# Strided attention products and softmax normalisations of chunks 2 to 4 on VectorE instead of GpSimd

## The chip, the cores and the metric

One core of a Trainium2 chip runs the kernel. The metric is the device time of one execution in microseconds (us). The engines are named as in the profile: PE is TensorE's matmul, PEld its weight load, DVE is VectorE, ACT is ScalarE, POOL is GpSimd, SP is SyncE, which here only issues DMAs.

## The reference

Three layers follow one another, all in 32-bit floats.

```python
# q, k, v: (4 batches, 8 heads, 576 positions, 64)
scores = scale * q @ k^T
mask_local   = (rel >= 0) & (rel < 32)                      # heads 0 to 3
mask_strided = (rel >= 0) & (pos_k % 32 == pos_q % 32)      # heads 4 to 7
attn = softmax(where(mask, scores, -1e9));  x = attn @ v    # x: (2304, 512)
g = x @ w_gate
x = (silu(g) * (x @ w_val)) @ w_out                         # 512 -> 1536 -> 512
h = max(x @ w1, x @ w2, x @ w3)                             # 512 -> 768
out = h @ w_out2                                            # 768 -> 512
```

A position of a strided head sees the positions of its own residue modulo 32 alone, at most 18 of them. With the 32 residues and the 4 heads laid over the 128 partitions, row i of a batch (i from 0 to 17) needs i+1 dot products of length 64 on each partition and then a weighted sum of i+1 vectors of length 64.

## The kernel before

**Chunks and slots.** The 2304 tokens are 72 rows of 32 positions. They are cut into five chunks of 15, 15, 14, 14 and 14 rows (480 or 448 tokens), called chunks 0 to 4. The gated layer runs chunk after chunk, and in each over twelve blocks f of 128 hidden columns. One (chunk, f) pair is a slot, written (c, f) here, 48 in all. A slot does a gate product (12 matmuls into the PSUM tile `ps_g`), a value product (12 into `ps_v`) and, one slot late, the output product of the slot before (into `ps_y`). Operands are split into a high and a low part (`hi`, `lo`; `xh`, `xl`; `hh`, `hl`), and a product is three matmuls.

**What a slot asks of the other engines.** ACT takes the tanh of `ps_g` (L524). DVE makes `ht` from it (L525) and multiplies it with `ps_v` (L532). ACT copies out the high part `hh` (L135), POOL subtracts for the low part `hl` (L138). `ps_g` and `ps_v` share two PSUM buffers (`gv`), so that the gate product of the next slot can start only when L525 of this slot has read `ps_g`, and the next value product only when L532 has read `ps_v`.

**The attention of the next chunk runs beside it.** `attention_steps(c)` gives lists of steps, and the main loop places list i of chunk c in slot 12(c-1)+i-3 (chunk 1: in slot i). There are two kinds of work:

- Blocks (class `Block`): local heads, and the first rows of the strided heads of batches 0 and 1, on PE, with a softmax (`softmax`): score, running minimum on DVE (L311), exponential on ACT (L315), sum and reciprocal on DVE (L318, L319), and the normalisation by `norm_eng` (L320). Then PE transposes the normalised tile (L325) and multiplies it with v (L339). Chunks 2 to 4 have four blocks each.
- Units (class `Unit`): the strided rows that are not on PE, in groups of up to six rows. For each row, `qk` multiplies k with the row's q (L416, into the tile `pr`), and DVE sums over the 64 columns (L419, into `stsc`). After the softmax of the unit, `pv` multiplies v with the weights (L438, into `pr`), and DVE sums (L441, into `sto`). `pr` has two buffers, `stsc` one. Chunk 1 has 2 such rows, chunks 2, 3 and 4 have 14 each, 42 together. A row of index i is a product over 64(i+1) columns, 64 to 1152.

`eng` names the engine of L416, L438 and of `norm_eng` at L320. It is DVE for chunk 1 and POOL for chunks 2 to 4.

**Other work in the same stretch.** In chunk 0 the weights of the gated layer are read as 64-bit words and converted to 32-bit floats (`convert`: L158, L159 on ACT, L160 on POOL, L161 on POOL or DVE, L162 and L163 on DVE) and split (L138). In slots of chunks 1 to 4 the weights of the last layers are converted and combined in the same way (`pair_steps`: L195 to L198, L207), paced by the list `PACE`. After slot (4, 9) the last two layers begin; the changed code has no part in them.

**Order.** The instructions of an engine stand in one queue and run in that order. A framework sorts them when the program is made, by program order and by when it expects each to be ready; the waits on semaphores then hold them to the data. Nothing in the diff names an order.

Of the kernel before, what the change touches and what calls it, by code (L numbers as in the profile page):

```python
# [59 lines left out]
def tile_attention_swiglu_maxout(  # L60
# [18 lines left out]
    nc = tc.nc  # L79
# [269 lines left out]
    def local_block(g, early=False):  # L349


        def dst(src):
            for c, i0, i1, o in pieces(LR * g[0], LR * (g[-1] + 1)):
                t, w = slice(i0 * STRIDE, i1 * STRIDE), slice(o * STRIDE, (o + i1 - i0) * STRIDE)
                xh, xl = x_tile(c)
                yield xh[:, 0:2, t], xl[:, 0:2, t], src[:, :, w]

        src = (earq if early else locq, lock, locv)
        return Block(src, (g[0] if early else g[0] - EARLY, g[0]), KB, [mask[0 if n % (NI // LR) == 0 else 1] for n in g], dst, early)

    def strided_block(srcs, b, g, early=False):

        _, rows, nr = ON_PE[b]

        def dst(src):
            for u, n in enumerate(g):
                r0 = min(n * nr, STRIDE - nr)
                su = src[:, :, u * QB:u * QB + nr * rows].rearrange("p a (r i) -> p a r i", i=rows)
                for c, i0, i1, o in pieces(b * NI, b * NI + rows):
                    def part(t):  # L370
                        t = t[:, 2:4, :width(c)].rearrange("p a (i r) -> p a r i", r=STRIDE)
                        return t[:, :, r0:r0 + nr, i0:i1]

                    xh, xl = x_tile(c)
                    yield part(xh), part(xl), su[:, :, :, o:o + i1 - i0]

        return Block(srcs, (g[0], g[0]), rows * nr, [smask[b]] * len(g), dst, early)

    def pairs(ns):
        ns = list(ns)  # L380
        return [ns[i:i + 2] for i in range(0, len(ns), 2)]
# [80 lines left out]
    def attention_steps(c):  # L462

        steps = [[] for _ in range(15)]
        a, b = ROWS[c], ROWS[c + 1]
        eng = nc.vector if c == 1 else nc.gpsimd
        blocks = [local_block(g) for g in pairs(g for g in range(-(-a // LR), -(-b // LR)) if g >= EARLY)]
        if a <= NI < b and len(ON_PE) > 1:
            blocks += [strided_block((st1q, st1k, st1v), 1, g) for g in pairs(range(-(-STRIDE // ON_PE[1][2])))]
        at = [0, 0, 4, 4, 8] if len(blocks) < 6 else [0, 0, 2, 2, 4, 4, 6, 6, 8]  # L470
        for n, blk in enumerate(blocks):
            s0 = at[n]
            steps[max(0, s0 - 2)].append(blk.load)
            steps[s0].append(lambda blk=blk: (blk.scores(), blk.softmax(eng)))
            steps[s0 + 1].append(lambda blk=blk: blk.transpose(nc.scalar))
            steps[s0 + 2].append(blk.pv)
        units = []
        on_pe = {n: rows for n, rows, _ in ON_PE}
        i = a
        while i < b:  # L480
            if i % NI < on_pe.get(i // NI, 0):
                i += 1
                continue
            n = min(6 - i % NI % 6, b - i)
            units.append(Unit(i // NI, i % NI, n))
            i += n
        s0 = 0
        for u in units:
            steps[s0].append(u.load)
            steps[s0].append(u.begin)  # L490
            for r in range(u.n):
                steps[s0 + (2 * r // u.n)].append(lambda u=u, r=r: u.qk(r, eng))
            steps[s0 + 2].append(u.softmax)
            for r in range(u.n):
                steps[s0 + 2 + (2 * r // u.n)].append(lambda u=u, r=r: u.pv(r, eng))
            for r in range(0, u.n, 3):
                steps[s0 + 5 + r // 3].append(lambda u=u, r=r: u.out(r))
            s0 += 4
        return steps
# [254 lines left out]
    if True:  # L754
# [26 lines left out]
        for c in range(1, NC):  # L781
            for i, st in enumerate(attention_steps(c)):
                fill.setdefault(i if c == 1 else (c - 1) * NF + i - 3, []).extend(st)
# [183 lines left out]
```

## Time and profile before

| | |
|---|---|
| median of 3 runs | 852.52 us (851.6 to 852.91) |
| the profiled execution | 851.26 us, of which 849.5 us are the span from its first to its last instruction |
| mean granted clock of TensorE | 0.992 |
| busy share of the span | PE 95%, PEld 83%, DVE 63%, ACT 39%, POOL 46% |
| chunk 0's slots | about 40 to 162 us |
| chunks 1, 2, 3 | begin at about 162, 278 and 374 us |
| chunk 4, then the last layers | begin at about 474 and 565 us |

A busy share is a mean over stages that differ. PE's busy time includes the latency of pipelined matmuls, so that a stretch in which PE stands at 100% can still hold short stalls. The profile tells for each instruction how long its engine sat idle before it, and which engine's instruction ended that idle time.

### The profile page before, as it was taken

What the parts mean: (1) busy time and instruction counts of PE and PEld (TensorE: products, weight loads), DVE (VectorE), ACT (ScalarE), POOL (GpSimd) and SP (SyncE); (2) the same over time, 40 slices, a digit from 0 to 9 for tenths busy, and PEclk for the clock granted to TensorE, in tenths of its full rate; (3) what the DMA queues carried; (4) which work ended last, traced back from release to release, by engine and by line L of the source; (5) the groups of instructions that cost most, each with busy time, mean ns of one, the idle gap of its engine ahead of it and who ended that gap; (6) DMA issues with size and microseconds to landing.
All of it is one profiled execution on the core that took longest, in us unless ns stands there. A gap on an engine that the chain in (4) does not pass through costs nothing.

```text
span 849.5 us, 12626 instructions
## 1 busy us (share of the span) xinstructions
PE 805.3 (95%) x4392; PEld 708.8 (83%) x4392; DVE 538.2 (63%) x1072; ACT 331.4 (39%) x811; POOL 387.7 (46%) x343
## 2 busy tenths in 40 slices
PE   4799899879999999999997999989999999999997
PEld 3677667658888989989896999889999899989986
DVE  3989999977675878847999553633645244524340
ACT  4867476343433443434232242422244123512220
POOL 0355455786666768755987343520313021302110
PEclk9899999989999999999999999999999999999999
DMA  8679778976865889858586996597766375644502
GB/s 234 216 223 378 235 250 292 399 243 220 285 207 164 276 311 305 286 187 287 175 261 226 316 328 213 178 351 320 247 239 219 132 277 225 219 189 148 212 0 75
DMA packets 73915, 202.72 MB, mean 239 GB/s; under 512 B 8716, under 2 KB 38472, under 8 KB 70268
## 3 DMA queue, kind: packets, MB, share of 16 engines
q1 hardware_dynamic: 73852, 201.92, 69.9%
q8 instruction: 35, 0.57, 0.3%
q14 instruction: 28, 0.23, 0.1%
HBM read 160.21 MB, written 41.68 MB: 238 GB/s over the span
## 4 chain that ended last, share of the span: by engine, by line
PE 68%; DVE 13%; DMA 6%; ACT 4%; POOL 4%; issue 4%; SPq 1%; DVEq 0%; ACTq 0%; POOLq 0%
PE ps_a L613 13%; PE ps_z L686 8%; PE ps_c L613 7%; PE ps_g L504 4%; PE ps_g L505 4%; PE ps_y L506 4%; PE ps_g L506 4%; PE ps_y L505 4%; PE ps_y L504 4%; PE ps_v L505 4%; PE ps_v L506 4%; PE ps_v L504 4%; PE ps_b L613 3%; POOL pr L416 2%; DVE w L162 2%
## 5 line engine op out<-in xcount | busy, mean ns | idle before, releaser
L138 POOL TENSOR_TENSOR hl<-t,hh 128x384 fp32r<-128x384 f32 x36 | 37.5, 1045 | 207.7 <-ACT hh L135 161.0
L504 PE MATMUL ps_g<-xh,wh_g 128*128 128x448 f32 (+1 forms) x240 | 94.2, 392 | 7.2 <-DVE ht L525 6.8
L138 POOL TENSOR_TENSOR hl<-ht,hh 128x448 fp32r<-128x448 f32 (+1 forms) x48 | 60.7, 1265 | 82.2 <-ACT hh L135 70.5
L613 PE MATMUL ps_a<-yhT,wr 128*128 128x384 f32 x324 | 94.4, 338 | 0.6 <-ACT s L627 0.6
L504 PE MATMUL ps_v<-xh,w_v 128*128 128x448 f32 (+1 forms) x240 | 89.7, 374 | 1.6 <-DVE stat L311 1.4
L505 PE MATMUL ps_g<-xl,wh_g 128*128 128x448 f32 (+1 forms) x240 | 89.6, 373 | 1.7 <-DVE xl L347 1.7
L506 PE MATMUL ps_g<-xh,wl_g 128*128 128x448 f32 (+1 forms) x240 | 89.9, 375 | 1.1 <-DVE wl_g L138 1.1
L506 PE MATMUL ps_v<-xh,w_v 128*128 128x448 f32 (+1 forms) x240 | 90.2, 376 | 0.0
L505 PE MATMUL ps_v<-xl,w_v 128*128 128x448 f32 (+1 forms) x240 | 89.1, 371 | 0.0
L160 POOL TENSOR_SCALAR raw<-raw 128x512 f32<-128x512 f32 x60 | 53.5, 893 | 61.6 <-ACT w L158 49.7
L627 ACT ACTIVATE s<-ps_a 128x384 f32<-128x384 f32 x81 | 39.3, 490 | 99.0 <-PE ps_a L613 96.1
L438 POOL TENSOR_TENSOR pr<-stv,stsc 128x832 f32<-128x832 f32 (+17 forms) x42 | 67.4, 1624 | 21.4 <-DVE sto L441 9.9
L416 POOL TENSOR_TENSOR pr<-stk,stq 128x832 f32<-128x832 f32 (+17 forms) x42 | 70.6, 1699 | 12.7 <-DVE sto L441 7.1
L506 PE MATMUL ps_y<-hh,w_o 128*128 128x448 f32 (+1 forms) x192 | 71.2, 371 | 0.0
L505 PE MATMUL ps_y<-hl,w_o 128*128 128x448 f32 (+1 forms) x192 | 71.0, 370 | 0.0
L504 PE MATMUL ps_y<-hh,w_o 128*128 128x448 f32 (+1 forms) x192 | 68.0, 373 | 0.0
L686 PE MATMUL ps_z<-wo2t,hh 128*128 128x512 f32 x216 | 64.8, 392 | 0.9 <-ACT osb L695 0.7
L135 ACT ACTIVATE hh<-ht 128x448 fp32r<-128x448 f32 (+1 forms) x48 | 28.0, 584 | 94.6 <-DVE ht L532 89.0
L524 ACT ACTIVATE ht<-ps_g 128x448 f32<-128x448 f32 (+1 forms) x60 | 33.1, 551 | 74.0 <-PE ps_g L506 70.2
L613 PEld LDWEIGHTS ps_a<-yhT,wr 128*128 128x128 f32 x324 | 59.7, 188 | 1.6 <-ACT s L627 1.0
L525 DVE SCALAR_TENSOR_TENSOR ht<-ht,ps_g 128x448 f32<-128x448 f32 (+1 forms) x60 | 37.6, 626 | 34.1 <-ACT ht L524 34.1
L504 PEld LDWEIGHTS ps_g<-xh,wh_g 128*128 128x128 f32 x240 | 45.3, 189 | 16.1 <-DVE ht L525 9.6
(133 smaller groups left out, 1956.5 us busy)
## 6 DMA issues: line engine op xcount, KB each, us to landing
wr<-wsdr SPq DMA_DIRECT2D x27, 1792.0 KB, 7.4
raw<-in_w_dram SPq DMA_DIRECT2D x60, 512.0 KB, 5.4
w_v<-wvdr SPq DMA_DIRECT2D x48, 512.0 KB, 4.4
w_o<-wodr SPq DMA_DIRECT2D x48, 512.0 KB, 4.7
wsdr<-whi SPq DMA_DIRECT2D x27, 256.0 KB, 3.9
wvdr<-w_v SPq DMA_DIRECT2D x12, 512.0 KB, 5.0
wodr<-w_o SPq DMA_DIRECT2D x12, 512.0 KB, 6.3
wsdr<-w SPq DMA_DIRECT2D x18, 256.0 KB, 4.1
```

The lines of the kernel that those rows point to most:

```text
L138: return a.ins, lo_eng.tensor_tensor(lo, src, f32(hi), ALU.subtract).ins
L160: nc.gpsimd.tensor_scalar(f32(hi), f32(hi), -0.0, 1.0, ALU.mult, ALU.mult)
L416: eng.tensor_tensor(pv, self.k[:, 0:i + 1, :], self.q[:, r:r + 1, :].to_broadcast([128, i + 1, D]), ALU.mult)
L438: eng.tensor_tensor(pv, self.v[:, :, 0:i + 1], self.sc[:, r:r + 1, 0:i + 1].to_broadcast([128, D, i + 1]), ALU.mult)
L504: nc.tensor.matmul(ps, wh, xh, start=first, stop=False)
L505: nc.tensor.matmul(ps, wh, xl, start=False, stop=False)
L506: nc.tensor.matmul(ps, wl, xh, start=False, stop=last)
L524: nc.scalar.activation(t, ps[:, :n], AF.Tanh, scale=0.5)
L525: nc.vector.scalar_tensor_tensor(t, t, 1.0, ps[:, :n], ALU.add, ALU.mult)
L613: nc.tensor.matmul(ps, wts[:, c, a, ks], y[k][b], start=first and k == q == 0, stop=k == 1 and q == 2, skip_group_check=True,)
L627: nc.scalar.activation(s, self.a, AF.Copy)
L686: nc.tensor.matmul(z[j], a[:, ts], w[:, f, b], start=f == q == 0, stop=f == NF2 - 1 and q == 2)
```

## The change

`eng` is DVE for every chunk. The products L416 and L438 of the 42 strided rows of chunks 2 to 4, 84 instructions, and the normalisations L320 of their twelve blocks go from POOL's queue to DVE's. Data, tiles and the number of instructions stay the same.

```diff
     def attention_steps(c):
 
         steps = [[] for _ in range(15)]
         a, b = ROWS[c], ROWS[c + 1]
-        eng = nc.vector if c == 1 else nc.gpsimd
+        eng = nc.vector
```

The steps that use it:

```python
steps[s0].append(lambda blk=blk: (blk.scores(), blk.softmax(eng)))
...
steps[s0 + (2 * r // u.n)].append(lambda u=u, r=r: u.qk(r, eng))
steps[s0 + 2].append(u.softmax)
...
steps[s0 + 2 + (2 * r // u.n)].append(lambda u=u, r=r: u.pv(r, eng))
```

## Rows read from the trace of the kernel before

**Rows 1.** The page's head: the span; busy us, share and instructions by engine.

```profile
span 849.5 us, 12626 instructions
PE 805.3 (95%) x4392; PEld 708.8 (83%) x4392; DVE 538.2 (63%) x1072; ACT 331.4 (39%) x811; POOL 387.7 (46%) x343
```

**Rows 2.** Stretches A, M, B: length, busy us (instructions): PE, PEld, DVE, ACT, POOL; clock; DMA.

```profile
151.10:199.60 48.50, 41.39 (x210) 31.50 (x209) 42.47 (x81) 16.95 (x51) 39.95 (x28) 0.93 0.85 302
199.60:407.20 207.60, 207.60 (x1154) 184.95 (x1153) 147.07 (x324) 81.02 (x212) 139.33 (x123) 1.00 0.77 251
407.20:474.40 67.20, 61.91 (x309) 54.90 (x308) 58.33 (x70) 19.23 (x42) 52.94 (x35) 1.00 0.72 238
```

**Rows 3.** What PE waited for, whole span: us in total, times, longest.

```profile
PE ps_g L504 <- DVE ht L525: 6.8, 9, 1.7
```

**Rows 4.** Timeline in slot (1, 7): start, us, engine, line; idle before, its releaser.

```profile
237.34 0.57 ACT L524 ACTIVATE ht<-ps_g 128x480 f32<-128x480 f32 x1 [2.76 <-PE ps_g L506]
237.95 0.65 DVE L525 SCALAR_TENSOR_TENSOR ht<-ht,ps_g 128x480 f32<-128x480 f32 x1 [1.27 <-ACT ht L524]
...
242.53 0.38 PE L504 MATMUL ps_g<-xh,wh_g 128*128 128x480 f32 x1
```

**Rows 5.** Timeline in slot (3, 8).

```profile
441.04 0.55 ACT L524 ACTIVATE ht<-ps_g 128x448 f32<-128x448 f32 x1 [0.59 <-PE ps_g L506]
...
441.86 4.65 POOL L438 TENSOR_TENSOR pr<-stv,stsc 128x832 f32<-128x832 f32 x2 [0.60 <-DVE stsc L431]
...
442.46 2.19 DVE L163 CUSTOM_DVE_ANT_0 w<-w,q 128x1024 uint16<-128x1024 uint16 x1
...
444.68 2.11 DVE L195 TENSOR_TENSOR s<-w 128x256 f32<-128x256 f32 x1
...
447.64 0.60 DVE L525 SCALAR_TENSOR_TENSOR ht<-ht,ps_g 128x448 f32<-128x448 f32 x1
...
448.30 0.47 PE L504 MATMUL ps_g<-xh,wh_g 128*128 128x448 f32 x1 [0.16 <-DVE ht L525]
```

**Rows 6.** Timeline in slot (1, 1): POOL and PE.

```profile
177.99 8.17 POOL L438 TENSOR_TENSOR pr<-stv,stsc 128x832 f32<-128x832 f32 x4 [0.86 <-POOL sm L320]
...
187.00 1.09 PE L325 MATMUL ps_a<-cst,sm 128*96 128x128 f32 x4 [4.76 <-POOL sm L320]
```

**Rows 7.** Stretches A, M, B: instructions on the tile pr: busy DVE, POOL; clock; DMA.

```profile
151.10:199.60 48.50, 15.99 (x18) 32.01 (x18) 0.93 0.85 302
199.60:407.20 207.60, 37.60 (x53) 72.28 (x52) 1.00 0.77 251
407.20:474.40 67.20, 16.11 (x15) 33.53 (x14) 1.00 0.72 238
```

**Rows 8.** Groups by shape, whole span: busy us, mean ns of one, idle before.

```profile
L416 DVE TENSOR_TENSOR pr<-stk,stq 128x1152 f32<-128x1152 f32 x1 | 1.3, 1342 | 0.0
...
L419 DVE TENSOR_REDUCE stsc<-pr 128x18 f32<-128x1152 f32 x4 | 5.4, 1342 | 0.0
...
L438 DVE TENSOR_TENSOR pr<-stv,stsc 128x1152 f32<-128x1152 f32 x1 | 1.8, 1784 | 0.0
...
L320 DVE TENSOR_TENSOR sm<-sm,stat 128x384 f32<-128x384 f32 x3 | 2.4, 818 | 0.0
```

**Rows 9.** Groups on DVE in stretch A.

```profile
L163 DVE CUSTOM_DVE_ANT_0 w<-w,q 128x1024 uint16<-128x1024 uint16 x4 | 4.4, 1100 | 0.0
L162 DVE SCALAR_TENSOR_TENSOR w<-w,raw 128x512 int32<-128x512 int32 x3 | 4.4, 1453 | 0.0
```

**Rows 10.** Groups on DVE in stretch B.

```profile
L163 DVE CUSTOM_DVE_ANT_0 w<-w,q 128x1024 uint16<-128x1024 uint16 x5 | 6.7, 1345 | 0.2
L161 DVE TENSOR_SCALAR w<-w 128x512 f32<-128x512 f32 x4 | 5.6, 1391 | 2.4 <-ACT w L158 2.4
```

**Rows 11.** Lines L163 and L161, whole span: ns shortest/median/longest, first and last start.

```profile
L163 DVE CUSTOM_DVE_ANT_0 w<-w,q x60: 673/685/2474, 28.5 to 542.1; 128x1024 uint16<-128x1024 uint16 x60
...
L161 DVE TENSOR_SCALAR w<-w x24: 417/937/2415, 190.5 to 539.7; 128x512 f32<-128x512 f32 x24
```

## The prediction

> **What bounds the kernel now.** I read the page's head first. PE is busy for 805.3 of the 849.5 us of the span, so that a gain or loss must come from where PE waits or would begin to wait [rows 1]. Then I cut the part in which POOL runs the strided products into three stretches at the boundaries of slots: A, 151.1 to 199.6 us, is slots (0, 11) to (1, 2); M, 199.6 to 407.2, is slots (1, 3) to (3, 3); B, 407.2 to 474.4, is slots (3, 4) to (3, 11). Together they are 323.3 us, and the change touches nothing outside them.
>
> The stretches differ [rows 2]. In M, PE is busy all the time and DVE for 147.1 of 207.6 us, 71%: PE is the bound. In A, PE is idle for 48.5 - 41.4 = 7.1 us and DVE is busy for 42.5, 88%; PE's granted clock falls to 0.93 on the mean after such idle time, from the upper of its two levels. In B, PE is idle for 67.2 - 61.9 = 5.3 us, DVE is busy for 58.3, 87%. So PE loses time just where DVE's queue is nearly full, and the list of PE's waits names the instruction: L525, the `ht` of the gate product, nine times, 6.8 us [rows 3].
>
> The reader should see how much room L525 has. In slot (1, 7) the tanh ends at 237.91, L525 starts 0.04 us later and ends at 238.60, and the gate product that needs the PSUM buffer starts at 242.53: 3.9 us to spare [rows 4]. In slot (3, 8) the tanh ends at 441.59, but DVE gets to L525 only at 447.64, and PE's next gate product starts at 448.30, released by it [rows 5]. What stands ahead of L525 there is two weight instructions of 2.19 and 2.11 us, both beside two POOL products of 4.65 us. L163 takes 0.685 us by its median [rows 11], so it lasted 1.5 us longer beside that POOL product.
>
> The Trainium skill has a rule for this (SBUF — State Buffer, Who interferes with whom): a DVE instruction with two SBUF inputs and a GpSimd instruction that reads SBUF exclude one another, and whichever comes second waits for the whole of the first. The 2.19 us in rows 5 agrees. It is weighed again below.
>
> POOL's queue costs PE one wait by itself. In slot (1, 1), four products L438 hold POOL for 8.17 us, the normalisation L320 of a block stands behind them, and PE's transposes wait 4.76 us for it [rows 6].
>
> **What goes from POOL.** The 84 products take 32.0 us of POOL in A, 72.3 in M and 33.5 in B, 137.8 in all [rows 7]; with the twelve normalisations POOL loses some 148 us. POOL is not the bound of any stretch, so this gives nothing by itself; it gives what waits for POOL.
>
> **What comes to DVE.** For a row of 1152 columns DVE's product L416 of chunk 1 took 1.342 us, the same as the sum L419 over these columns. L438 took 1.784 [rows 8]. I price each new product like the sum that follows it, so that the added time is the DVE time on `pr` that each stretch already shows: 16.0 us in A, 37.6 in M, 16.1 in B, 69.7 together [rows 7]. If half of them (the L438) cost 1.784/1.342 = 1.33 times as much, 11.5 us more are added; I take the lower value, since L438's two instructions in chunk 1 stand among POOL's weight work and L416's are nearer to the price of a plain pass. The twelve normalisations cost at most 0.82 us each [rows 8]: 1.6 us for two of them in A, 8.2 for ten in M.
>
> **What DVE gets back.** Instructions that now wait beside POOL's products become shorter. In A, L163 and L162 (both over 512 32-bit columns, so both judged by L163's 0.685 us) exceed that by 4 x 0.415 + 3 x 0.768 = 4.0 us [rows 9, 11]. In B, L163 exceeds it by 5 x 0.66 = 3.3, and L161 exceeds its shortest, 0.417, by 4 x 0.974 = 3.9: 7.2 us [rows 10, 11]. Both are lower bounds, since other lines (L195 of rows 5) show the same; the upper bound is POOL's time that goes, which is far off. Part of the excess stays, because POOL keeps its `hl` and weight instructions. I take 6 us in A and 10 in B, and keep 4 to 9 and 7 to 16 for the range.
>
> By the Trainium skill's rule of exclusion all of this excess could go where only products stood beside it. By that rule alone B would be left with 58.3 + 16.1 - 16 = 58 us of DVE work, and the rival below is priced by it.
>
> **The sum.** A: 42.5 + 16.0 + 1.6 - 6 = 54.1 us of DVE work in a stretch of 48.5. PE's wait of 4.76 us for the normalisation goes, but the normalisation now stands in DVE's queue among the same L438 and L441, so that the wait moves and is not saved. 5.6 us too many: what is not urgent can slip into M, which has room, but the program puts this work ahead of the `ht` of later slots, so I let half of it slip: +3 us. M: 147.1 + 37.6 + 8.2 = 192.9 of 207.6 us before any relief. PE stays the bound and hides it; the cover is the 3.9 us that L525 has to spare, and what it costs if that goes is the next rival. I add 1 us for single late L525. B: 58.3 + 16.1 - 10 = 64.4 of 67.2 us. DVE stays as full as it was, with products of 1.3 us in place of blocked instructions of 2 us and more; of PE's 5.3 idle us I expect 1 back. Elsewhere: 0. Sum +3 us on the profiled execution's 851.26, which is 1.3 below the median of the runs; on the median, 855.5.
>
> No DMA moves with the change, and SP's queue is not passed. The loads of a unit wait for buffers as before. What is queued behind a product on DVE: L525 and L532 of the next slots, and so PE; the weight conversions, which have slots to spare.
>
> **Rivals.** (1) Faster: the waits go and nothing takes their place. For it speaks that DVE's long instructions in B stand just beside POOL's products [rows 5], and that in M the `ht` is served at once [rows 4]. Against it, A's DVE work exceeds A. If A loses its PE idle time of 7.1 us but for 2, and B its 5.3 but for 2, the gain is 8.4: 844 on the median. It decides if A's surplus of 5.6 us slips into M, which has 207.6 - 192.9 = 14.7 us of DVE room, and L525 there starts within the 3.9 us.
>
> (2) No change: A's surplus is absorbed in part, B gives back as much. 851 to 854. It needs A's loss to be under 2 us.
>
> (3) Clearly slower: DVE fills up in M too. It stands at 93% there by the sum, and 139.3 - 72.3 = 67 us of POOL's work stay in M, some 58 without the normalisations [rows 2, 7]. If a fifth of these 58 us holds up the new products, 12 us, M has 192.9 + 12 = 204.9 of 207.6 us, as full as B and fuller; B loses PE 5.3 in 67.2, 8%, so that a third of M in that state costs 69 x 0.08 = 5.5 us. With A's whole 5.6 us that is +11: 864.
>
> By the rule of the Trainium skill named above, the products on DVE have two SBUF inputs and would be held by every POOL instruction that reads SBUF; this is the mechanism of (3), and no row of before shows how often it would meet.
>
> **How the numbers follow.** A measurement of this kernel can tell 0.2%, 1.7 us, from no change. My case, +2 to +8 us, has 0.37; (3) has 0.10; (2) has 0.20; (1) has 0.33. So slower 0.47, same 0.20, faster 0.33. The likeliest is +3, 855.5; by itself its range is 854 to 861. Since both signs hold much, the range goes from near (1), with up to 10 us gained, to (3): 842 to 865.
>
> **What would show it.** Right: `pr` products of about 1.3 us per 1152 columns on DVE; DVE over 95% in A and A about 51 us long; L163 in B near 0.7 us; M near 90% DVE with PE busy throughout; L525 late by more than 3.9 us in a few slots. Wrong: A shorter than 47 us, or chunk 4 beginning well before 474 us while A is no longer; that is (1). M longer than 210 us is (3). If the products cost 1.33 times the sums, A grows by more than 3 us. A new order of the instructions, made for the new prices, can also move a wait to a place that no row here shows.

## The result, and the profile after

The change made the kernel faster: 840.08 us median of 4 runs (838.6 to 841.09) against 852.68 (851.6 to 852.91) for the kernel before on the same chip, ratio 0.9853 with a 95% interval of 0.9835 to 0.9872. The forecast was 855.5 and slower, and 840.08 lies below its whole range of 842 to 865; what happened is its rival (1), which gave 844. The profiled execution took 838.6 us.

The head of the page after, to be held against [rows 1]:

```profile
span 836.8 us, 12646 instructions
PE 802.8 (96%) x4392; PEld 707.4 (85%) x4392; DVE 581.0 (69%) x1168; ACT 330.7 (40%) x811; POOL 248.3 (30%) x247
```

POOL lost 139 us, DVE gained 43 and PE's own busy time fell by 2.5. The same three stretches, cut at the first gate product of slots (0, 11), (1, 3), (3, 4) and (4, 0); columns as in [rows 2]:

```profile
149.70:191.90 42.20, 39.80 (x215) 30.70 (x213) 41.84 (x76) 14.37 (x41) 5.80 (x8) 1.00 0.89 331
191.90:400.00 208.10, 208.10 (x1158) 184.77 (x1158) 189.91 (x414) 81.44 (x220) 63.26 (x61) 1.00 0.77 254
400.00:462.60 62.60, 60.72 (x301) 54.78 (x301) 58.69 (x81) 20.87 (x44) 22.36 (x20) 1.00 0.73 247
```

A is 6.3 us shorter (48.5 to 42.2), B 4.6 (67.2 to 62.6), M 0.5 longer. That is 10.4 of the 12.7 us by which the span fell. The rest is 1.4 in the start, before the first slot, and about 1 after B, where the change touches nothing; the start alone lies between 37.5 and 40.0 us in most kernels of this study, so I leave it as scatter. In A, PE's idle time fell from 7.1 to 2.4 us, and its busy time by 1.6 for the same slots, with a granted clock of 1.00 against 0.93. In B, its idle time fell from 5.3 to 1.9 us and its busy time by 1.2, with the clock at 1.00 both times. In A, DVE is busy for 41.84 of the 42.20 us.

The tile `pr` in these stretches, for [rows 7]; now all of it is DVE's:

```profile
149.70:191.90 42.20, 24.98 (x22) 1.00 0.89 331
191.90:400.00 208.10, 91.92 (x123) 1.00 0.77 254
400.00:462.60 62.60, 27.84 (x24) 1.00 0.73 247
```

Of A's 36 instructions on `pr` (18 products, 18 sums) 22 are left in A; 14 slipped into M. PE's waits, whole span, without those for DMA, beside [rows 3]:

```profile
PE ps_g L504 <- DVE ht L525: 5.7, 7, 1.7
...
PE ps_v L504 <- DVE ht L532: 1.9, 3, 1.2
```

The wait for L525 is nearly as long as before, although I had named it as the one that counts. Of its 6.8 us before, only 1.4 lay in A and 1.6 in B; the other 3.8 lay outside both. After, 1.8 lie in A, 0.2 in B and 3.7 outside. Two other waits are gone: the 4.76 us for the normalisation in A [rows 6], and one of B that I did not put among my rows. PE's waits inside B, before:

```profile
PE ps_a L448 <- DVE sto L441: 3.7, 3, 2.1
PE ps_g L504 <- DVE ht L525: 1.6, 4, 0.7
```

and after:

```profile
PE ps_v L504 <- DVE ht L532: 1.6, 2, 1.2
PE ps_g L504 <- DVE ht L525: 0.2, 1, 0.2
```

The transposes of the units' outputs (L448) waited for sums of the unit (L441). In slot (3, 8), which I read in [rows 5], PE's timeline before had this line just ahead of the gate product:

```profile
447.87 0.27 PE L448 MATMUL ps_a<-cst,sto 128*64 128x128 f32 x1 [2.06 <-DVE sto L441]
```

PE had stood 2.06 us there, and then 0.16 for L525. Both instructions were late for the same reason, but the transpose was the one that PE stood at. None of the three sums that L448 waited for was late for its own product: DVE did not sit idle before any of them. Each stood in DVE's queue behind a weight instruction that lasted long beside a product on POOL: L195 with 2.11 us [rows 5], L207 with 2.78 and L161 with 2.42, where the shortest of each in this kernel are 0.41, 0.86 and 0.42. The second and the third on DVE, POOL and PE, before:

```profile
452.57 2.75 POOL L438 TENSOR_TENSOR pr<-stv,stsc 128x1024 f32<-128x1024 f32 x1
...
453.09 2.78 DVE L207 TENSOR_TENSOR s<-s,whi 128x512 f32<-128x512 f32 x1
...
455.79 1.14 DVE L441 TENSOR_REDUCE sto<-pr 128x64 f32<-128x960 f32 x1
...
456.99 0.30 PE L448 MATMUL ps_a<-cst,sto 128*64 128x128 f32 x1 [0.93 <-DVE sto L441]
...
460.31 2.42 DVE L161 TENSOR_SCALAR w<-w 128x512 f32<-128x512 f32 x1 [1.20 <-ACT w L158]
...
462.91 1.27 DVE L441 TENSOR_REDUCE sto<-pr 128x64 f32<-128x1088 f32 x1
...
464.24 0.30 PE L448 MATMUL ps_a<-cst,sto 128*64 128x128 f32 x1 [0.67 <-DVE sto L441]
```

The product that the second sum reads, over 960 columns, had started at 447.80 and taken 2.15 us.

Slot (1, 1) after, on DVE and PE, for [rows 6]:

```profile
175.08 0.55 DVE L320 TENSOR_TENSOR sm<-sm,stat 128x384 f32<-128x384 f32 x1
...
176.13 0.56 DVE L320 TENSOR_TENSOR sm<-sm,stat 128x384 f32<-128x384 f32 x1
...
177.64 2.03 DVE L438 TENSOR_TENSOR pr<-stv,stsc 128x832 f32<-128x832 f32 x2
179.59 2.01 DVE L441 TENSOR_REDUCE sto<-pr 128x64 f32<-128x832 f32 x2
181.51 0.65 DVE L525 SCALAR_TENSOR_TENSOR ht<-ht,ps_g 128x480 f32<-128x480 f32 x1
...
182.21 0.48 PE L504 MATMUL ps_g<-xh,wh_g 128*128 128x480 f32 x1 [0.50 <-DVE ht L525]
```

Both normalisations stand ahead of the products now; before, the second stood behind four of them. L525 is released after two products and two sums, and PE waits 0.50 us. The slot takes 10.9 us where it took 16.5.

Prices by shape, whole span:

```profile
L320 DVE TENSOR_TENSOR sm<-sm,stat 128x384 f32<-128x384 f32 x12 | 6.5, 552 | 0.1
L438 DVE TENSOR_TENSOR pr<-stv,stsc 128x1152 f32<-128x1152 f32 x4 | 5.8, 1458 | 0.0
L416 DVE TENSOR_TENSOR pr<-stk,stq 128x1152 f32<-128x1152 f32 x4 | 5.4, 1352 | 0.0
L419 DVE TENSOR_REDUCE stsc<-pr 128x18 f32<-128x1152 f32 x4 | 5.4, 1343 | 0.0
```

and in B the weight groups of [rows 10]:

```profile
L163 DVE CUSTOM_DVE_ANT_0 w<-w,q 128x1024 uint16<-128x1024 uint16 x5 | 4.4, 877 | 0.0
...
L161 DVE TENSOR_SCALAR w<-w 128x512 f32<-128x512 f32 x5 | 3.1, 634 | 1.0 <-ACT w L158 1.0
```

### The profile page after: what moved, and what is told of

The parts are those of the page before. It is cut to its first block, busy times and chain, and to the rows that moved or that the text cites. A ratio compares the mean times of both kernels' runs of the same rounds, so it can differ in the third digit from the quotient of the medians.

```text
span 836.8 us, 12646 instructions
## 1 busy us (share of the span) xinstructions
PE 802.8 (96%) x4392; PEld 707.4 (85%) x4392; DVE 581.0 (69%) x1168; ACT 330.7 (40%) x811; POOL 248.3 (30%) x247
## 4 chain that ended last, share of the span: by engine, by line
PE 69%; DVE 16%; DMA 7%; issue 4%; ACT 2%; POOL 1%; SPq 1%; DVEq 0%; POOLq 0%; ACTq 0%
PE ps_a L613 13%; PE ps_z L686 9%; PE ps_c L613 7%; PE ps_v L506 4%; PE ps_v L504 4%; PE ps_v L505 4%; PE ps_g L504 4%; PE ps_g L506 4%; PE ps_y L504 4%; PE ps_g L505 4%; PE ps_y L505 4%; PE ps_y L506 4%; PE ps_b L613 3%; DVE pr L438 2%; DVE stsc L419 1%
## 5 line engine op out<-in xcount | busy, mean ns | idle before, releaser
L504 PE MATMUL ps_g<-xh,wh_g 128*128 128x448 f32 (+1 forms) x240 | 93.4, 389 | 6.1 <-DVE ht L525 5.7
L504 PE MATMUL ps_v<-xh,w_v 128*128 128x448 f32 (+1 forms) x240 | 90.1, 376 | 3.5 <-DVE ht L532 1.9
L160 POOL TENSOR_SCALAR raw<-raw 128x512 f32<-128x512 f32 x60 | 56.8, 950 | 59.2 <-ACT w L158 49.0
L506 PE MATMUL ps_y<-hh,w_o 128*128 128x448 f32 (+1 forms) x192 | 70.9, 369 | 0.0
L504 PE MATMUL ps_y<-hh,w_o 128*128 128x448 f32 (+1 forms) x192 | 63.5, 374 | 0.0
L504 PEld LDWEIGHTS ps_g<-xh,wh_g 128*128 128x128 f32 x240 | 45.1, 188 | 14.4 <-DVE ht L525 7.9
L613 PE MATMUL ps_a<-ylT,wr 128*128 128x384 f32 x162 | 54.8, 338 | 0.0
L504 PEld LDWEIGHTS ps_v<-xh,w_v 128*128 128x128 f32 x240 | 45.1, 188 | 10.1 <-DVE ht L532 3.0
L525 DVE SCALAR_TENSOR_TENSOR ht<-ht,ps_g 128x448 f32<-128x448 f32 (+1 forms) x60 | 37.6, 626 | 21.4 <-ACT ht L524 21.3
```

What stands on the lines that cost most here:

```text
L160: nc.gpsimd.tensor_scalar(f32(hi), f32(hi), -0.0, 1.0, ALU.mult, ALU.mult)
L504: nc.tensor.matmul(ps, wh, xh, start=first, stop=False)
L506: nc.tensor.matmul(ps, wl, xh, start=False, stop=last)
L525: nc.vector.scalar_tensor_tensor(t, t, 1.0, ps[:, :n], ALU.add, ALU.mult)
L613: nc.tensor.matmul(ps, wts[:, c, a, ks], y[k][b], start=first and k == q == 0, stop=k == 1 and q == 2, skip_group_check=True,)
```

## The experiments

My theory after the result: the gain is made in A and B alone, each by its own chunk; in A it comes from the order of the queues and the sums that no longer wait for POOL, in B from instructions that POOL's reads no longer hold up. The rivals: POOL's queue (the normalisations behind products) is all of it; or POOL's reads are all of it, in both stretches. All kernels are compared with the kernel before on the same chip; A, M and B are us of the profiled execution, cut at the same slots. "Ratio" is to the kernel before.

| kernel | median us | ratio (95%) | A | M | B |
|---|---|---|---|---|---|
| before | 852.68 | 1 | 48.5 | 207.6 | 67.2 |
| after | 840.08 | 0.9853 (0.9835 to 0.9872) | 42.2 | 208.2 | 62.6 |
| norm_only | 856.9 | 1.0055 (1.0037 to 1.0074) | 52.3 | 208.0 | 68.9 |
| prod_only | 843.03 | 0.989 (0.9872 to 0.9909) | 43.6 | 208.7 | 63.1 |
| chunk2_only | 845.23 | 0.9916 (0.9899 to 0.9933) | 42.4 | 207.3 | 67.2 |
| chunk4_only | 848.79 | 0.9955 (0.9936 to 0.9975) | 49.8 | 208.2 | 63.3 |
| pool_reads | 898.96 | 1.0551 (1.053 to 1.0572) | 48.7 | 225.6 | 62.5 |
| pool_writes | 843.95 | 0.9902 (0.9879 to 0.9925) | 42.2 | 206.3 | 62.6 |
| qk_only | 845.01 | 0.9921 (0.9902 to 0.994) | 40.0 | 212.8 | 65.0 |
| pv_only | 856.64 | 1.0061 (1.0037 to 1.0084) | 51.5 | 207.3 | 69.9 |
| norm_first | 847.93 | 0.9957 (0.9941 to 0.9973) | 45.5 | 207.1 | 67.3 |
| reads_b | 868.1 | 1.0183 (1.0156 to 1.0211) | 42.4 | 215.3 | 84.1 |
| m_double | 852.23 | 0.9998 (0.9986 to 1.0011) | 42.9 | 219.1 | 64.1 |
| l161_pool | 842.73 | 0.9889 (0.9864 to 0.9913) | 42.4 | 209.3 | 64.1 |

**The change by kind of work.** Only the normalisations moved, and only the products moved:

```diff
 # norm_only, against before
-            steps[s0].append(lambda blk=blk: (blk.scores(), blk.softmax(eng)))
+            steps[s0].append(lambda blk=blk: (blk.scores(), blk.softmax(nc.vector)))
 # prod_only, against before
-                steps[s0 + (2 * r // u.n)].append(lambda u=u, r=r: u.qk(r, eng))
+                steps[s0 + (2 * r // u.n)].append(lambda u=u, r=r: u.qk(r, nc.vector))
...
-                steps[s0 + 2 + (2 * r // u.n)].append(lambda u=u, r=r: u.pv(r, eng))
+                steps[s0 + 2 + (2 * r // u.n)].append(lambda u=u, r=r: u.pv(r, nc.vector))
```

> Only the twelve normalisations L320 of chunks 2 to 4 go to DVE; the 84 products stay on POOL. Theory Q (POOL's queue: the gain came because normalisations and sums no longer stand behind products in POOL's queue): PE's 4.76 us wait for L320 goes, A shrinks from 48.5 to about 43 us, B stays at 67 us, total about 847. Theory L (exclusion: the gain came because DVE's instructions no longer wait beside POOL's products): products stay, so A and B stay within 1.5 us and the total is 851 to 854.

> Only the 84 products go to DVE; the normalisations stay on POOL. Theory Q and theory L both expect the whole gain (POOL's queue is short and no product on POOL excludes DVE): A about 42, B about 63 us, total 839 to 842. If the total is 846 or more, the normalisation's engine itself carries part of the gain.

The normalisations alone make the kernel slower, which neither theory had forecast, and the products alone bring three quarters of the gain. So it is not enough that the normalisations leave POOL's queue. In norm_only the wait did just what my prediction said it would: it moved. The timeline of slot (1, 1) there:

```profile
177.74 8.15 POOL L438 TENSOR_TENSOR pr<-stv,stsc 128x832 f32<-128x832 f32 x4 [3.14 <-issue]
179.68 1.02 DVE L441 TENSOR_REDUCE sto<-pr 128x64 f32<-128x832 f32 x1 [2.08 <-POOL pr L438]
...
182.66 1.06 DVE L318 TENSOR_SCALAR stat<-stat 128x4 f32<-128x4 f32 x1
...
183.97 2.34 DVE L320 TENSOR_TENSOR sm<-sm,stat 128x384 f32<-128x384 f32 x1
...
186.46 1.06 PE L325 MATMUL ps_a<-cst,sm 128*96 128x128 f32 x4 [4.90 <-DVE sm L320]
```

DVE's queue has the second block's minima, L318 and L320 behind sums that wait for POOL's products; L320 itself lasts 2.34 us beside a product, 0.55 when nothing of POOL stands beside it. PE waits 4.90 us, against 4.76 before.

**The change by chunk.**

```diff
 # chunk2_only, against after
-        eng = nc.vector
+        eng = nc.vector if c <= 2 else nc.gpsimd
 # chunk4_only, against after
-        eng = nc.vector
+        eng = nc.vector if c in (1, 4) else nc.gpsimd
```

> DVE for the attention of chunks 1 and 2 alone; chunks 3 and 4 stay on POOL. If the stretches are independent: A loses its 6.3 us as in the changed kernel, B stays at 67 us: 846 to 847. If the gain comes of a new order of the whole program, the stretches do not add up so.

> DVE for the attention of chunks 1 and 4 alone; chunks 2 and 3 stay on POOL. If the stretches are independent: A stays at 48.5 us, B goes from 67.2 to about 62.6: 847 to 848. With the sum of the two single-chunk gains near 11 of the whole 12.6 us, chunk 3's part (M) is near nothing.

Chunk 2's part makes A short and leaves B at 67.2; chunk 4's part makes B short and leaves A long. The gains of the ratios, 0.84% and 0.45%, add up to 1.29%, the whole change's 1.47% with its interval of 1.28 to 1.65. Chunk 3's part, which lies in M, is worth nothing that shows.

**POOL reading, POOL only writing.** Both kernels are the one after plus, for each of the 84 products, work on POOL that nothing needs (one instruction in pool_reads, two in pool_writes; none is left out). It is issued behind the product, writes as many columns into a scratch tile, and either reads a constant twice or reads nothing:

```diff
 # pool_reads, against after
+            nc.gpsimd.tensor_tensor(d, c, c, ALU.mult)
 # pool_writes, against after
+            nc.gpsimd.memset(d, 0.0)
+            nc.gpsimd.memset(d, 0.0)
```

> The changed kernel, and on POOL, beside each of the 84 products that DVE now does, an additional product of the same size on constants into a tile that nobody reads: POOL reads SBUF as much as before the change, but nothing waits for it. Theory L (exclusion): DVE's instructions with two SBUF inputs last as long as before the change again (L163 up to 2.4 us, L195 up to 2.1 us), A and B lose most of their 6.3 and 4.6 us, total 848 us or more, well above it if the new products themselves are held up (84 times up to 2.5 us). Theory P (pace: the gain came of products that last 1.3 instead of 2.6 us and of no hand-over between POOL and DVE): total 840 to 842.

> As the kernel with additional products on POOL, but in place of each additional product two fills of the same tile with zero: POOL is busy about as long and its queue is as full, but it reads nothing from SBUF. Theory L: 840 to 843 us, DVE's instructions as short as in the changed kernel. If the queue of POOL (hl behind the additional work) is what costs, this kernel is as slow as the one with additional products.

The added instructions keep POOL busy for 125.9 us in the one and 109.8 in the other, so that POOL's queue is about equally full. The times lie 55.0 us apart: some 59 us over the kernel after with reads, some 4 without (by the ratios to before, which was run again beside each, the same to 1 us). DVE's busy time is 635.6 us with reads and 580.2 with fills, against 581.0 after. What grew is not what theory L named: L195 lasts up to 1.04 us there, not 2.1, but the products L416 on DVE last up to 2.95 us against 1.71 after. What costs is that POOL reads, and not that it is busy. Where it costs is less clear than I meant it to be: having only a constant to wait for, the dummies ran early, 63.9 us of them before A and none in B, and B is the same 62.5 us in both. In pool_writes, A, M and B are no longer than after, and its extra time lies before A. So the pair says nothing on B.

**One half of the products on each engine.**

```diff
 # qk_only, against after
-                steps[s0 + 2 + (2 * r // u.n)].append(lambda u=u, r=r: u.pv(r, eng))
+                steps[s0 + 2 + (2 * r // u.n)].append(lambda u=u, r=r: u.pv(r, nc.vector if c == 1 else nc.gpsimd))
 # pv_only, against after
-                steps[s0 + (2 * r // u.n)].append(lambda u=u, r=r: u.qk(r, eng))
+                steps[s0 + (2 * r // u.n)].append(lambda u=u, r=r: u.qk(r, nc.vector if c == 1 else nc.gpsimd))
```

> The products of qk and the normalisations on DVE, the products of pv of chunks 2 to 4 stay on POOL. In slot (1, 1) PE waited for a normalisation that came late beside four products of pv, and in slot (3, 8) the long DVE instructions stood beside products of pv. So theory L and theory P expect little gain: A stays at 46 us or more, B at 65 or more, total 848 to 853.

> The products of pv and the normalisations on DVE, the products of qk of chunks 2 to 4 stay on POOL. By the same places most of the gain should come with pv: A 42 to 44 us, B 62 to 65, total 840 to 845.

These I expected the wrong way round. With L416 on DVE and L438 on POOL, A is at its shortest, 40.0 us, but part of that is paid in M, and A and M together are 252.8 us against 250.4 after; with L438 on DVE and L416 on POOL, the kernel is slower than before, though POOL reads far less. In pv_only's slot (1, 1), on DVE, POOL and PE:

```profile
175.39 1.23 POOL L138 TENSOR_TENSOR hl<-ht,hh 128x480 fp32r<-128x480 f32 x1 [1.06 <-ACT hh L135]
...
179.67 2.03 DVE L438 TENSOR_TENSOR pr<-stv,stsc 128x832 f32<-128x832 f32 x2
181.61 2.01 DVE L441 TENSOR_REDUCE sto<-pr 128x64 f32<-128x832 f32 x2
...
184.24 2.29 DVE L438 TENSOR_TENSOR pr<-stv,stsc 128x960 f32<-128x960 f32 x2
...
188.79 1.26 DVE L438 TENSOR_TENSOR pr<-stv,stsc 128x1088 f32<-128x1088 f32 x1
189.97 0.65 DVE L525 SCALAR_TENSOR_TENSOR ht<-ht,ps_g 128x480 f32<-128x480 f32 x1
...
190.67 0.77 PE L504 MATMUL ps_g<-xh,wh_g 128*128 128x480 f32 x1 [7.09 <-DVE ht L525]
...
191.95 0.13 POOL L410 MEMSET stsc<- 128x36 f32 x1 [15.32 <-DVE pr L438]
```

POOL does nothing from 176.6 to 191.95, each product runs at its clean price, and yet PE waits 7.09 us: L525 stands behind five products and four sums (and the block's four minima and L318), where after has it behind two and two. This is a loss by order alone, and it is as large as A's whole gain. In B, the same kernel shows the hold-up: a weight instruction beside a product, with L525 behind it.

```profile
435.55 3.07 POOL L416 TENSOR_TENSOR pr<-stk,stq 128x1152 f32<-128x1152 f32 x1
436.07 3.09 DVE L207 TENSOR_TENSOR s<-s,whi 128x512 f32<-128x512 f32 x1
...
439.75 0.74 PE L504 MATMUL ps_g<-xh,wh_g 128*128 128x448 f32 x1 [5.20 <-DVE ht L525]
```

**The order with the engines of before.** norm_first has every instruction on the engine of the kernel before; only, the `pv` products of chunk 2's first unit are tied behind the second block's normalisation in POOL's queue:

```diff
 # norm_first, against before
         def pv(self, r, eng):
+            if (self.b, self.i0) == (1, 12):
+                with tc.issue_after(tie[0]):
+                    return self.pv_(r, eng)
+            return self.pv_(r, eng)
...
+        if c == 2:
+            steps[0].append(lambda: tie.append(norms[-1]))
```

> The kernel before the change, all products and normalisations on POOL, with one tie in the order: the products of pv of the first unit of chunk 2 are put behind the normalisations of the two blocks of that chunk that run beside it. Theory O (order: A's gain came because the minima and the normalisation of the second block moved ahead of the products of pv, in the queues): A 41 to 44 us in place of 48.5, M and B as before, total 845 to 848. Theory L (exclusion in A): A stays at 47 us or more, total 850 to 853.

A is 45.5 us: the order alone gives 3.0 of A's 6.3, and the kernel is faster than before by 0.27% to 0.59%. That ends the rival that POOL's reads are all of it in A, as the same instructions still read on POOL. Nor is POOL's queue all of it, as the normalisations ahead of the products bring 0.43% of the 1.47%. The 3.0 is rough: chunk4_only, with the same engines in A, had 49.8 us where before had 48.5. The two normalisations run at 176.44 and 181.00, and PE's wait for L320 is gone. What is left is here (in its numbering L446 is the product L438, L449 the sum L441, L535 is L525 and L514 is L504):

```profile
183.71 1.02 DVE L449 TENSOR_REDUCE sto<-pr 128x64 f32<-128x832 f32 x1 [2.89 <-POOL pr L446]
...
184.98 0.64 DVE L535 SCALAR_TENSOR_TENSOR ht<-ht,ps_g 128x480 f32<-128x480 f32 x1
...
185.68 0.48 PE L514 MATMUL ps_g<-xh,wh_g 128*128 128x480 f32 x1 [1.46 <-DVE ht L535]
```

DVE itself stands idle for 2.89 us at a sum that waits for a POOL product, with L525 queued behind it. The tie has a part in this: it holds the first product back to 181.78, where it started at 177.99 before. On DVE, a product and its sum stand one after the other and this wait can't arise.

**POOL's reads in B.** reads_b is the kernel after, with each product of chunk 4 made a second time on POOL, from the same inputs, into a scratch tile:

```diff
 # reads_b, against after, in qk (and likewise in pv)
+            if self.b * NI + i >= ROWS[4]:
+                nc.gpsimd.tensor_tensor(
+                    dummy[:, :(i + 1) * D].rearrange("p (j d) -> p j d", d=D), self.k[:, 0:i + 1, :],
+                    self.q[:, r:r + 1, :].to_broadcast([128, i + 1, D]), ALU.mult
+                )
```

> The changed kernel, with an additional product on POOL beside each product of chunk 4 that DVE does (28 of them, same operands, into a tile that nobody reads), so that POOL reads SBUF in B as before the change. Theory L for B (exclusion): DVE's weight instructions in B get long again and B goes from 62.6 us to 67 or more, above the 67.2 of before, since the products on DVE are held up too; A stays at 42. Theory P (pace): B stays within 1.5 us of 62.6.

B grows from 62.6 to 84.1 us. Its row in the view of stretches, and the copies on POOL alone:

```profile
409.00:493.10 84.10, 68.31 (x300) 60.01 (x301) 80.67 (x84) 21.19 (x44) 53.05 (x32) 0.90 0.53 175
```

```profile
409.00:493.10 84.10, 30.73 (x12) 0.90 0.53 175
```

30.7 us of reading on POOL make DVE's busy time 80.67 - 58.69 = 22.0 us longer, with 84 instructions against 81. DVE's one wait there is 1.2 us, for PE, so it does not wait for the copies' data. PE waits for DVE at L525 and L532, 17.5 us, and its clock falls to 0.90. M is 7.1 us longer too; 25.7 us of the copies fell there. One place, first DVE, then POOL (L445 on DVE and L449 on POOL are its two products of the kind L438; its L438 is the last step of the unit's softmax):

```profile
449.23 2.10 DVE L162 SCALAR_TENSOR_TENSOR w<-w,raw 128x512 int32<-128x512 int32 x1
451.25 5.77 DVE L445 TENSOR_TENSOR pr<-stv,stsc 128x832 f32<-128x832 f32 x2
```

```profile
448.87 7.20 POOL L449 TENSOR_TENSOR dummy<-stv,stsc 128x832 f32<-128x832 f32 x3 [1.27 <-DVE stsc L438]
```

Two products that took 2.03 us in the kernel after take 5.77, and the weight instruction ahead of them 2.10. This is the mechanism of my rival (3); the change escapes it only because it takes the products away from POOL altogether.

**How much room M has.** m_double makes chunk 3's products twice, both on DVE:

```diff
 # m_double, against after
-            eng.tensor_tensor(
+            for _ in range(2 if ROWS[3] <= self.b * NI + i < ROWS[4] else 1):
+                eng.tensor_tensor(
```

> The changed kernel with every product of chunk 3 done twice on DVE, some 31 us more work for DVE in M, which is at 190 of 208 us there. If M's cover is DVE's idle time, 18 us, M grows by at least 13 us; if PE already loses time below that, by more. The total then is 852 to 860. If M grows by less than 8 us, work slips out of M or DVE had more room than its busy time shows.

I expected 13 us or more in M if its cover were DVE's idle time, less than 8 if it had more room. M's instructions on `pr` go from 123 to 149 and DVE's busy time there from 189.9 to 210.9 us. M grows by 10.9:

```profile
193.90:413.00 219.10, 211.42 (x1159) 186.01 (x1158) 210.87 (x439) 81.20 (x219) 68.03 (x61) 0.99 0.73 241
```

M's cover was 208.1 - 189.9 = 18.2 us of DVE on the mean. 21 us more do not cost the 2.8 by which they exceed it but 10.9, as they fall on a few slots: from 260 to 300 us DVE is busy for 40.00 of 40 us, and PE is idle for 3.8 us of the second half of these. So M was within some 20 us of being the loss that rival (3) described.

**One more instruction to POOL.** With POOL idle for 70% of the span, L161 of all weights goes there:

```diff
 # l161_pool, against after
-        eng = nc.gpsimd if key[0] in ("g", "v", "o") else nc.vector
+        eng = nc.gpsimd
```

> The changed kernel with the clamp L161 of the last layers' weights on POOL, which is idle for most of the time now: 24 instructions, about 18 us, off DVE. If DVE's work sets B and the start of M, B shrinks by 1 to 3 us: total 837 to 840. By exclusion POOL's additional reads hold up products on DVE: then no gain or a loss of 1 to 3 us.

842.73 us, no better than the kernel after. In B, L161 takes 0.82 us on POOL where DVE took 0.63, and DVE's busy time stays at 58.9 us. Its L163 lasts 0.94 us instead of 0.88. Filling POOL with work that reads gives DVE nothing. No version here beats the kernel after.

## Why the prediction was wrong

**The step that failed: A, "+3 us".** It had two parts. The first was that "the wait moves and is not saved": by norm_only this holds when the products stay on POOL (4.90 us against 4.76), but not with the products on DVE. Products and normalisations then stand in one queue, and the framework put both L320 ahead of the first L438. I read the order of the trace before as if it would stay, and only named a new order in my last sentence. norm_first shows that this order is worth 3.0 of A's 6.3 us with nothing else changed. Of the other 3.3, PE's idle time makes 1.7 (4.1 us in norm_first, 2.4 after) and its busy time 1.5, with a granted clock of 0.96 against 1.00; norm_first's trace shows in that place a sum that waits for POOL's product, with L525 behind it (in A before, DVE stood idle for 5.6 us at such sums). The second part was the surplus, of which "I let half of it slip", 2.8 us; 14 of the 36 instructions on `pr` slipped into M, and of the 32.0 us that I had put on `pr` in A (twice 16.0) only 24.98 were left, so that 7.0 slipped. DVE is full in A, as I said (41.84 of 42.20 us), but with work that nobody waits for. A full engine cost PE 1.8 us at L525 in A, where the same wait had cost 1.4 before, as little of what PE needs stood at its queue's end.

**B, "of PE's 5.3 idle us I expect 1 back".** 3.4 us of PE's idle time came back and 1.2 of its busy time. My DVE sum was 58.3 + 16.1 - 10 = 64.4; it came to 58.69. On `pr` DVE has 27.84 us in B against 16.11, so 11.7 were added and not 16.1 (24 instructions on `pr` are left in B where there were 29), and all the rest fell from 42.2 to 30.9 us, by 11.4 and not 10. The Trainium skill's rule (SBUF — State Buffer, Who interferes with whom) gave 58 for this sum; the total agrees by luck, as its terms, 16.1 added and 16 off, don't. What the sum missed in any case is which wait went: PE stood at L448 for 3.7 us in B, at L525 for 1.6, and with DVE as busy as before (58.69 us) PE waited for it 1.8 us.

**What held.** Rival (1) let 2 us of PE's idle time stay in each stretch; 2.4 stayed in A and 1.9 in B. It lies 4 us too high since it left out PE's busy time, 2.8 us less in A and B, and the 2.3 outside. M: +0.5 us against my +1, with DVE at 189.9 us against my 192.9, and m_double shows that the cover was real and nearly used up. The price of L416: 1.352 us against 1.342 forecast. L438: 1.458, between my 1.342 and 1.784. L320: 0.55 us, under my bound of 0.82. What DVE gets back: weight instructions shortened as forecast, L163 in B from 1.345 to 0.877 us and L161 from 1.391 to 0.634. What POOL keeps in B, 22.4 us, still holds a product now and then: the L416 over 896 columns took 1.53 us there, the one over 1024 columns 1.21.

**What stays open.** Of A's gain, how much of the 3.3 us is sums that wait for POOL and how much is instructions held up by its reads was not tried by itself. In B, that the gain comes of instructions no longer held up is read from the trace of before and borne out by reads_b, which puts POOL's reads back; no run takes away the holding up alone. pv_only (69.9 us) undoes more than the whole gain in B and qk_only (65.0) half of it, by different waits, so that the shares of the two kinds of products can't be added there.

## What to carry to other kernels

When work changes its engine, ask which instructions it will stand before in the new queue, and look for the one that PE waits for: the same products on DVE cost 7.1 us of PE in one order and 0.5 in another. A stretch in which the receiving engine is full is no loss by itself if its surplus can slip behind what the bound needs; work out where it slips to, and how much room is left there. Before a wait is named, look for all the waits of the bound in that stretch, as the last one ahead of a long gap hides those that PE stood at first.

## What the hardware showed

VectorE was slowed by what GpSimd read, though the two had little to do for each other. 84 added POOL instructions that read cost 55.0 us more than fills of the same tiles, at about the same busy time, and in B 30.7 us of POOL reading added 22.0 us to DVE, with three instructions more there. Which DVE instructions are held was sharper than I had expected. Before, those with two SBUF inputs were (L163 up to 2.47 us, 0.69 its median), and so was L161, which has one (up to 2.42, shortest 0.42); L318, on four columns, took 1.07 us beside a product against its median of 0.17. The sums over 1152 columns were not: L419's mean stayed at 1.342 before and 1.343 after. The Trainium skill (SBUF — State Buffer, Who interferes with whom) says of this that a reduction never contends and that a `tensor_scalar` can; the rows agree.
